# A filter fold in three vector operations for six, and a product unit split by output block, in a gated mix of an FFT convolution and a mixer MLP

## Chip, cores, metric

The kernel runs on one core of a Trainium2 chip. The metric is the device time of one execution in microseconds (us). Five engines work side by side, each through its own list of instructions in order: TensorE (PE in the profile; its weight loads are PEld), VectorE (DVE), ScalarE (ACT), GpSimd (POOL) and SyncE (SP). SP and POOL also issue DMAs; an instruction waits on semaphores for what other engines and DMAs have to finish first.

## What is computed

Two branches over a sequence of S = 2048 rows and D = 640 columns share the input `A_q`, and a gate mixes them. Branch A is a long convolution, branch B a mixer with an MLP. `ssm_k` is a filter of 2048 taps for each of the 640 columns. Cut to what matters:

```python
def A(q, k, v, shift_k, ssm_k, ssm_D):
    k_shift = sum(pad(k, ks-1)[t:t+S] * shift_k[:, ks-1-t] for t in range(ks))   # ks = 4 taps
    kv  = k_shift * v
    y_f = rfft(pad(kv, S)) * rfft(pad(ssm_k, S))      # along the sequence, length 2S
    y   = irfft(y_f)[:S] + kv * ssm_D                 # bf16
    return q * y

def B(x, w1, w2, w3, w4):
    h  = gelu(layernorm(x) @ w1)
    hs = shift_four_column_groups(h, by=(1, -1, 2, -2)) @ w2
    x1 = x + hs
    return x1 + gelu(layernorm(x1) @ w3) @ w4

g   = sigmoid((A_q * gate_w).sum(-1))
out = g * A(A_q, ...) + (1 - g) * B(A_q, ...)
```

## The kernel before

All tensors live in one SBUF arena, so the profile calls nearly every operand `arena`; PSUM is `PSall`. Columns are worked in five chunks of 128 (c = 0 to 4).

Branch A, per chunk. `h_load` brings the filter of 128 columns, `h_fold` adds and subtracts mirrored halves of each block of 512 taps (so that a transform of half the length does), and a DMA transpose turns the result. The skip term `ssm_D` is folded into tap 0 of the filter. `h_even` folds a second time, `h_chunk` multiplies by small DFT matrices on TensorE and ScalarE copies the spectra from PSUM into `HF`. `kv` applies the four taps and the product with v, `kv2` and `x_fwd` do the same transform for the data into `XF`, and `combine` adds neighbouring blocks on VectorE. `x_fwd` has four parts of the spectrum, j = 0 to 3; the operation of `combine` for the lower half reads j = 0 and 1, that for the upper half 2 and 3. `unit(c)` then multiplies the spectra: there are four input blocks and four output blocks, and output block o sums the products over input blocks 0 to o. Complex products are made from three real ones. It works on pairs of output blocks, first (2, 3), then (0, 1): a product of the first filter block, then for each further one a product into `TT` and an addition into `ACC`, and last two operations and one copy of a single row that write the pair back into `XF`. Five of the additions are not VectorE operations but accumulating DMAs issued by POOL, chosen by a table. `final(g, o, q, k)` does the inverse transform on TensorE for a group g of chunks (0 to 2, or 3 and 4) and output block o, mirrors a half by a matmul with a flipped identity, multiplies by q and the gate and stores.

Branch B. `ln1`, `mm1` (w1 and gelu; the four shifted column groups are written into `hT` with their shift, the last 32 columns of each by a small copy), `mm2` (w2; a VectorE operation with PSUM input adds the residual and sums the row, line 980), `ln2`, `mm3` (w3 and gelu), `mm4` (w4, scaled by 1 - g); `base` stores a part of the rows that `mm4` then accumulates into.

What sets the order: the program records all operations with what they read and write, and `schedule` lays them out by `SEQUENCE`, a table of 1171 operation numbers that stands in the program. Each engine executes its operations in that order. `PLACES` gives each PSUM tile its bank. `ON` is a string of choices, one per place where the code calls `turn`: a scaling or a copy of a row on ScalarE or on VectorE, an addition on VectorE or as an accumulating DMA, a copy into `hT` on VectorE or as a DMA. Semaphore waits follow from the recorded dependences alone.

Most VectorE operations are issued by one helper, `tt` (line 660; `ts` is line 665), most ScalarE ones by `act` (670), most matmuls by `mm` (692), nearly all DMAs by line 237. Operations are therefore told apart by their shapes. Those that matter below: the first fold's large operations are 128x1016 (written 128x8x127 in the order), `combine` is 128x1536 (128x3x2x256), `unit` uses 128x2048, 128x1024, 128x3072, 128x1536 and 128x512 operations, `final` 128x256, 128x384, 128x512 and 128x768 ones.

Of the kernel before, what the change touches and what calls it, by code (L numbers as in the profile page):

```python
# [407 lines left out]
def _folded_dft():  # L408
# [22 lines left out]
            np.where(first, np.sin(np.pi * kodd / 2), -np.sin(w * 2 * kodd * p))]  # L431
    alt, one = (-1.) ** p, p == 0
    even[0][:, 0:1], even[1][:, 0:1] = (alt - 1) / 2, 0
    even[2][:, 0:1], even[3][:, 0:1] = one, (alt + 1) / 2
# [12 lines left out]
def bass_gated_mix__ssm_conv_h3__mixer_s_mlp__prompt_kernel(  # L447
# [34 lines left out]
    def ps(n, cls):  # L482
# [3 lines left out]
    SEQUENCE = [1, 4, 5, 6, 26, 7, 3, 45, 24, 8, 0, 49, 50, 51, 55, 48, 68, 9, 10, 11, 12, 13, 14, 15, 16, 69, 17,  # L486
# [682 lines left out]
```

## Time and profile before

| what | value |
|---|---|
| time, median of 3 runs | 221.62 us (221.31 to 222.36) |
| the profiled execution, its own time | 222.27 us |
| its span, first to last instruction | 220.2 us |
| granted TensorE clock, mean | 0.986 |
| VectorE in its first 10 us | 7.53 us busy |
| TensorE in its first 10 us | 6.98 us busy |
| DMA moved | 37.73 MB, mean 171 GB/s |

The profile is of one execution. A row of the groups by form gives line, engine, operation, output and input, shape, count, then busy time and mean duration (ns) of one, then idle time of the engine just before and what ended it. A row of stretches gives start and end, width, and for PE, PEld, DVE, ACT and POOL the busy time and the count, then the granted clock, the DMA share and GB/s. A row in order of time gives start, duration, engine, line and shape; consecutive instructions of one line may be merged into one row. A row of the chain of waits gives start, duration and who held the chain.

### The profile page before, as it was taken

To read this page: it belongs to the slowest core of one execution; us is meant where nothing else is said; L and a number is where in the kernel's file an instruction comes from. 1 tells how busy PE (TensorE), PEld (TensorE's weight loads), DVE (VectorE), ACT (ScalarE), POOL (GpSimd) and SP (SyncE) were. 2 spreads that over 40 slices of the span, in tenths; PEclk is the share of its full clock that TensorE was granted. 3 is DMA by queue.
4 is the path that set the end of the run, shared out by engine and by line. 5 is a ranking of instruction groups with operands and counts; after the bars stand their busy time and mean duration, and the time that the engine had idled before them with its cause. 6 is when DMAs were issued, how large, how long until landed. Compare 5 with 4: busy or idle time off the path is not lost.

```text
span 220.2 us, 3837 instructions
## 1 busy us (share of the span) xinstructions
PE 209.0 (95%) x1401; PEld 125.7 (57%) x1410; DVE 212.1 (96%) x418; ACT 196.5 (89%) x326; POOL 45.7 (21%) x48
## 2 busy tenths in 40 slices
PE   6899999999999999999999999999999999999961
PEld 2598755554664446665446565456665445776730
DVE  5999999999999999999999999999999998999993
ACT  2499999999999999999999999999798978558981
POOL 1331102400010001001380103331101060645440
PEclk9999999999999999999999999999999999999995
DMA  6999998999979995898486893793198299366696
GB/s 170 346 233 214 246 207 231 177 236 193 284 246 204 383 198 95 162 174 185 120 147 110 201 193 43 163 174 71 19 160 182 65 219 246 39 74 71 74 179 119
DMA packets 79440, 37.73 MB, mean 171 GB/s; under 512 B 59001, under 2 KB 76990, under 8 KB 79422
## 3 DMA queue, kind: packets, MB, share of 16 engines
q1 hardware_dynamic: 73920, 31.91, 63.3%
q0 software_dynamic: 5328, 5.51, 18.9%
q8 instruction: 11, 0.18, 0.3%
q10 hardware_dynamic: 174, 0.07, 0.2%
q14 instruction: 7, 0.06, 0.1%
HBM read 14.88 MB, written 5.77 MB: 94 GB/s over the span
## 4 chain that ended last, share of the span: by engine, by line
DVE 57%; PE 28%; DMA 5%; ACT 5%; issue 3%; SPq 0%
DVE arena L660 46%; PE PSall L692 28%; ACT arena L670 5%; DVE arena L665 4%; DMA arena<-arena 3%; DVE arena L861 3%; DVE arena L980 2%; DMA arena<-in_A_q_dram 2%; DVE arena L946 1%; DVE arena L862 0%; DVE arena L866 0%; SPq L237 0%; DVE arena L735 0%; DVE arena L704 0%
## 5 line engine op out<-in xcount | busy, mean ns | idle before, releaser
L692 PE MATMUL PSall<-arena 128*128 128x512 bf16 (+5 forms) x1340 | 201.7, 309 | 3.4 <-ACT arena L670 1.3
L660 DVE TENSOR_TENSOR arena<-arena 128x1024 bf16<-128x1024 bf16 (+14 forms) x270 | 175.1, 712 | 1.7 <-DMA arena<-arena 0.9
L692 PEld LDWEIGHTS PSall<-arena 128*128 128x128 bf16 x1349 | 121.6, 98 | 82.7 <-ACT arena L670 3.3
L670 ACT ACTIVATE arena<-PSall 128x512 bf16<-128x512 f32 (+7 forms) x157 | 94.1, 659 | 9.6 <-PE PSall L750 4.9
L670 ACT ACTIVATE arena<-arena 128x640 bf16<-128x640 bf16 (+5 forms) x107 | 93.5, 904 | 1.9 <-DVE arena L660 1.8
L237 POOL DMA_DIRECT2D out_dram<-arena x24 | 24.1, 1133 | 67.7 <-ACT arena L670 51.7
L869 POOL TENSOR_TENSOR arena<-arena 128x2 f32<-128x2 f32 (+2 forms) x15 | 17.3, 1157 | 58.0 <-DVE arena L866 42.3
L670 ACT ACTIVATE arena<-PSall,arena 128x640 bf16<-128x640 f32 (+2 forms) x32 | 20.5, 652 | 6.8 <-PE PSall L692 6.6
L237 POOL DMA_DIRECT2D arena<-arena x5 | 4.9, 978 | 43.2 <-DVE arena L660 43.2
L980 DVE SCALAR_TENSOR_TENSOR arena<-PSall,arena 128x640 bf16<-128x640 f32 x16 | 12.9, 816 | 0.3
L665 DVE TENSOR_SCALAR arena<-arena 128x640 bf16<-128x640 bf16 (+6 forms) x35 | 11.9, 358 | 0.1
L861 DVE BATCH_NORM_STATS2 arena<-arena 128x6 f32<-128x320 bf16 x20 | 9.0, 484 | 1.3 <-DMA arena<-in_A_q_dram 1.3
L715 PE MATMUL PSall<-arena 128*128 128x512 bf16 x15 | 5.4, 529 | 2.2 <-DVE arena L712 2.2
L670 ACT ACTIVATION_READ_ACCUMULATOR arena<-arena 128x1 f32 x28 | 5.7, 204 | 0.0
L946 DVE TENSOR_SCALAR arena<-arena 32x256 bf16<-32x256 bf16 (+1 forms) x22 | 5.3, 240 | 0.4
L715 PEld LDWEIGHTS PSall<-arena 128*128 128x128 bf16 x15 | 1.8, 128 | 5.0 <-issue 2.5
L922 PE MATMUL PSall<-arena 128*128 128x128 bf16 x40 | 3.4, 220 | 0.9 <-DVE arena L665 0.9
L922 PEld LDWEIGHTS PSall<-arena 128*128 128x128 bf16 x40 | 2.4, 97 | 1.3 <-DVE arena L665 1.3
L866 DVE SCALAR_TENSOR_TENSOR arena<-arena 128x2 f32<-128x2 f32 (+2 forms) x19 | 2.9, 155 | 0.0
L718 ACT ACT_TABLE_LOAD x1 | 1.3, 1283 | 1.3 <-PEq L1154 1.3
L862 DVE BATCH_NORM_AGGREGATE arena<-arena 128x2 f32<-128x12 f32 x10 | 1.7, 192 | 0.0
L980 DVE DVE_READ_ACCUMULATOR arena<-PSall,arena 128x1 f32 x16 | 1.3, 80 | 0.0
(19 smaller groups left out, 2.9 us busy)
## 6 DMA issues: line engine op xcount, KB each, us to landing
arena<-in_A_ssm_k_dram SPq DMA_DIRECT2D x5, 512.0 KB, 5.2
arena<-in_A_q_dram SPq DMA_DIRECT2D x6, 320.0 KB, 5.7
arena<-in_B_w_dram SPq DMA_DIRECT2D x1, 1920.0 KB, 8.4
out_dram<-arena SPq DMA_DIRECT2D x16, 96.0 KB, 3.9
arena<-arena POOLq DMA_DIRECT2D x4, 384.0 KB, 5.0
out_dram<-arena POOLq DMA_DIRECT2D x16, 96.0 KB, 3.6
arena<-in_A_q_dram SPq DMA_DIRECT2D x8, 192.0 KB, 4.1
out_dram<-arena POOLq DMA_DIRECT2D x8, 192.0 KB, 4.0
```

Of the source, the lines that this page charges most:

```text
L237: fn = lambda e: e.dma_start(out, in_, **kw)
L660: P.op(eng, lambda e: e.tensor_tensor(o, real(a), real(b), op), [a, b], [o], dve_ns(o, [a, b], 2) if eng == "dve" else 500)
L665: P.op(eng, lambda e: e.tensor_scalar(o, real(a), s1, s2, op0=op0, **({} if op1 is None else {"op1": op1})), [a] + aps, [o], dve_ns(o, [a] ...
L670: P.op("act", lambda e: e.activation(real(o), real(a), f, bias=bias, scale=scale, **({"accum_out": accum} if accum is not None else {})), ...
L692: fns.append(lambda e, l=l, r=r, i=i: e.matmul(real(o), l, r, start=(i == 0), stop=(i == last)))
L715: P.op("pe", lambda e: e.matmul(real(pw), warm[:, 0:128], warm[:, 128:640], start=True, stop=True), [warm], [pw], 427.0 if i < 14 else 216.0)
L861: P.op("dve", lambda e, o=o, i=i: e.bn_stats(o, i), [i], [o], 400)
L866: P.op("dve", lambda e: e.scalar_tensor_tensor(o, a, x, b, op0=op0, op1=op1), [a, b] + aps, [o], n_of(o) / 0.96 + 65)
L869: P.op("pool", lambda g: g.tensor_tensor(o, a, e, ALU.pow), [a, e], [o], dur)
L922: P.op("pe", [lambda e, c=c, pb=pb, xn=xn: e.transpose(real(pb)[:, 128 * c:128 * (c + 1)], xn[:, 128 * c:128 * (c + 1)], ident) for c in r ...
L946: P.op("dve", lambda e, o=hT[q, 4, c0:c0 + n], i=hx[q, :]: e.tensor_scalar(o, i, 1.0, None, op0=ALU.mult), [hx[q, :]], [hT[q, 4, c0:c0 + n ...
L980: P.op("dve", lambda e: e.scalar_tensor_tensor(x, real(pr), 1.0, x, op0=ALU.mult, op1=ALU.add, accum_out=st[1, 0][:, t:t + 1]), [pr, x], [ ...
```

## The change

`h_fold` had six VectorE operations per chunk: one adds `ssm_D` to tap 0, two each for the sum and the difference (127 columns of eight pieces, and column 128), and one scalar operation that copies column 0 of both halves. Now the sum and the difference take one operation each, over 128 columns of eight pieces, written as one run that starts at element 1; the last column of each piece then falls on column 0 of the next one, and a third operation overwrites those columns and adds `ssm_D`, held in a small tile `skip` with zeros between. The run of the fifth output ends one element beyond the tile, so each chunk's part of the arena is 16 elements longer (`HS`). One column of the difference changes its sign, which two rows of the DFT tables undo. `unit` for the fifth chunk (`LAST`) treats its last pair of output blocks (0, 1) as two single blocks, 1 and then 0. The VectorE copies into `hT` now also name the column beside them as an input. `SEQUENCE` (1163 numbers now), `PLACES` and `ON` are all new.

```diff
+    even[5][0] *= -1
...
+    odd[1][0] *= -1
...
-    SEQUENCE = [1, 4, 5, 6, 26, 7, 3, 45, 24, 8, 0, 49, 50, 51, 55, 48, 68, 9, 10, 11, 12, 13, 14, 15, 16, 69, 17,
...
+    SEQUENCE = [5, 26, 1, 29, 28, 4, 3, 8, 9, 7, 2, 47, 10, 27, 11, 0, 6, 12, 13, 14, 15, 16, 17, 52, 42, 18, 44, 40,
...
-    ON = ("0000000011111111011011111111111100010000010000101111000000000000001000010010000100000100000100000000"
-          "0000000000000000000000000000000")
-
-    HW = S + 4
+    ON = ("0000000011111111111111111111111100010000010000101111000000000000001000010010000100000100000100000000"
+          "00000100000000000000000000000000")
+
+    HW, HS = S + 4, 4096 + 16
...
-    dgT = bfs[:, 32:42]
-    Dcol, gwT = dgT[:, 0:5], dgT[:, 5:10]
+    skip = bfs[:, 0:40].rearrange("p (c e b) -> p c e b", c=5, e=2)
+    gwT = bfs[:, 48:53]
...
+    P.op("dve", lambda e: e.memset(skip, 0.0), [], [skip], 70)
...
-    act(dgT, pr, ACTF.Copy)
+    act(skip[:, :, 1, 0], pr[:, 0:5], ACTF.Copy)
+    act(gwT, pr[:, 5:10], ACTF.Copy)
...
         k, fo = kst[c], kfo[c]
-        tt(k[:, 0, 0:1], k[:, 0, 0:1], Dcol[:, c:c + 1], ALU.add)
         kh = k.rearrange("p b (h i) -> p b h i", h=2)
-        fh = fo.rearrange("p e b (h i) -> p e b h i", h=2)
         for e, op in ((0, ALU.add), (1, ALU.subtract)):
-            tt(fh[:, e, :, :, 1:128], kh[:, :, :, 1:128], kh[:, :, ::-1, 255:128:-1], op)
-            tt(fo[:, e, :, 128], k[:, :, 384], k[:, :, 128], op)
-        ts(fo[:, :, :, 0], kh.rearrange("p b h i -> p h b i")[:, ::-1, :, 0], 1.0, None, ALU.mult)
+            f = fo[:, e, :, 1:129]
+            tt(bass.AP(f.tensor, f.offset, [f.ap[0], [256, 4], [128, 2], [1, 128]]), kh[:, :, :, 1:129], kh[:, :, ::-1, 255:127:-1], op)
+        tt(fo[:, :, :, 0], kh.rearrange("p b h i -> p h b i")[:, ::-1, :, 0], skip[:, c], ALU.add)
...
-                         [hx[q, :]], [hT[q, 4, c0:c0 + n]], n / 3.84 + 65)
+                         [hx[q, :], hT[q, 4, c0 - 1:c0]], [hT[q, 4, c0:c0 + n]], n / 3.84 + 65)
...
-    ADDS = ()
+    ADDS, LAST = (), 4
...
-        for o0 in (2, 0):
-            for a in range(o0 + 2):
+        for o0, o1 in ((2, 4), (0, 2)) if c < LAST else ((2, 4), (1, 2), (0, 1)):
+            for a in range(o1):
                 lo = max(o0, a)
-                n, x0 = o0 + 2 - lo, lo - a
-                acc, tmp = ACC[:, lo - o0:2], TT[:, 0:n]
+                n, x0 = o1 - lo, lo - a
+                acc, tmp = ACC[:, lo - o0:o1 - o0], TT[:, 0:n]
...
-            Y = XF[:, c, o0:o0 + 2]
-            tt(Y[:, :, 0], ACC[:, :, 2], ACC[:, :, 1], ALU.subtract)
-            tt(Y[:, :, 1], ACC[:, :, 2], ACC[:, :, 0], ALU.add)
-            scale(Y[0:1, :, :, 0:128], ACC[0:1, :, 0:2, 0:128], 1.0, True)
+            Y, R = XF[:, c, o0:o1], ACC[:, 0:o1 - o0]
+            tt(Y[:, :, 0], R[:, :, 2], R[:, :, 1], ALU.subtract)
+            tt(Y[:, :, 1], R[:, :, 2], R[:, :, 0], ALU.add)
+            scale(Y[0:1, :, :, 0:128], R[0:1, :, 0:2, 0:128], 1.0, True)
```

Three places of the orders. (All line numbers behind `tt` are higher by one in the changed program.) The first is VectorE at the fold of chunk 0, about 14 us in; BN_STATS and BN_AGGR are the statistics of `ln1`, lines 946 and 947 the copies into `hT`. Before:

```order
L660 TENSOR_TENSOR arena<-arena 128x1
L660 TENSOR_TENSOR arena<-arena 128x4
L946 TENSOR_SCALAR arena<-arena 32x256
L861 BN_STATS arena<-arena 128x6
L665 TENSOR_SCALAR arena<-arena 128x2
L660 TENSOR_TENSOR arena<-arena 128x8x127
L861 BN_STATS arena<-arena 128x6
L660 TENSOR_TENSOR arena<-arena 128x8x127
L665 TENSOR_SCALAR arena<-arena 128x640 x2
L946 TENSOR_SCALAR arena<-arena 32x256
L665 TENSOR_SCALAR arena<-arena 128x8
```

Now:

```order
L862 BN_STATS arena<-arena 128x6 x4
L666 TENSOR_SCALAR arena<-arena 128x640 x2
L947 TENSOR_SCALAR arena<-arena 32x256
L661 TENSOR_TENSOR arena<-arena 128x1024 x2
L863 BN_AGGR arena<-arena 128x2
L661 TENSOR_TENSOR arena<-arena 128x8
```

The fold stands behind four statistics and two normalisations, in one piece, with one operation between its second and third.

The second is VectorE where unit 3 ends and unit 4 begins, about 175 us in. The first row, 128x2x1024, is the product whose sum POOL makes by an accumulating DMA; the last row, 128x2x512, is the first operation that reads that sum. The two 128x3x2x256 are the combines of chunk 4 (before: upper half, then lower; now the same), the 128x384 belong to `final`. Before:

```order
L660 TENSOR_TENSOR arena<-arena 128x2x1024
L660 TENSOR_TENSOR arena<-arena 128x3x2x256
L660 TENSOR_TENSOR arena<-arena 128x384 x2
L660 TENSOR_TENSOR arena<-arena 128x2048
L660 TENSOR_TENSOR arena<-arena 128x3x2x256
L660 TENSOR_TENSOR arena<-arena 128x384
L660 TENSOR_TENSOR arena<-arena 128x4x512
L660 TENSOR_TENSOR arena<-arena 128x384
L660 TENSOR_TENSOR arena<-arena 128x2048
L660 TENSOR_TENSOR arena<-arena 128x2x512
```

Now:

```order
L661 TENSOR_TENSOR arena<-arena 128x2x1024
L661 TENSOR_TENSOR arena<-arena 128x384 x2
L661 TENSOR_TENSOR arena<-arena 128x3x2x256
L661 TENSOR_TENSOR arena<-arena 128x384
L661 TENSOR_TENSOR arena<-arena 128x3x2x256
L661 TENSOR_TENSOR arena<-arena 128x2048
L661 TENSOR_TENSOR arena<-arena 128x384
L661 TENSOR_TENSOR arena<-arena 128x4x512
L661 TENSOR_TENSOR arena<-arena 128x384
L661 TENSOR_TENSOR arena<-arena 128x2048
L661 TENSOR_TENSOR arena<-arena 128x2x512
```

There is one more 128x384 between the product and the reader, and the second combine stands ahead of the 128x2048 that it followed.

The third is ScalarE, in the stretch whose copies the combines of chunk 4 read. The 128x2x4x128 are copies of spectra from PSUM (`h_chunk` and `x_fwd` of chunk 4), the 128x512 the gelus of `mm3`, the 128x384 scalings, the 1x4x128 a row of a unit. Before; the last 128x2x4x128 is the last part of `x_fwd`:

```order
L670 ACTIVATE arena<-PSall 128x2x4x128 x2
L670 ACTIVATE arena<-arena 128x384
L670 ACTIVATE arena<-PSall 128x2x4x128
L670 ACTIVATE arena<-PSall 128x512 x2
L670 ACTIVATE arena<-PSall 128x2x4x128
L670 ACTIVATE arena<-arena 128x384
L670 ACTIVATE arena<-arena 1x4x128
L670 ACTIVATE arena<-PSall 128x2x4x128
```

Now, from the last copy of `h_chunk` to the last of `x_fwd`:

```order
L671 ACTIVATE arena<-PSall 128x2x4x128
L671 ACTIVATE arena<-arena 128x384
L671 ACTIVATE arena<-PSall 128x512 x2
L671 ACTIVATE arena<-PSall 128x2x4x128
L671 ACTIVATE arena<-arena 128x384
L671 ACTIVATE arena<-PSall 128x2x4x128
L671 ACTIVATE arena<-arena 1x4x128
L671 ACTIVATE arena<-PSall 128x512
L671 ACTIVATE arena<-PSall 128x2x4x128
L671 ACTIVATE arena<-PSall 128x512
L671 ACTIVATE arena<-PSall 128x2x4x128
```

The parts of `x_fwd` now stand behind and between four gelus, not two, and on TensorE behind five groups of `mm3` matmuls, not three.

More of the change, by code (lines that the diff above doesn't have):

```diff
@@ L484, in ps @@
         return v if n == 1 else v.rearrange("p (b n) -> p b n", b=2)
-    SEQUENCE = [1, 4, 5, 6, 26, 7, 3, 45, 24, 8, 0, 49, 50, 51, 55, 48, 68, 9, 10, 11, 12, 13, 14, 15, 16, 69, 17,
[59 rows of a table removed]
-    PLACES = [4, 1, 7, 6, 5, 4, 6, 1, 1, 7, 0, 6, 3, 0, 2, 1, 3, 2, 3, 6, 7, 2, 1, 2, 7, 3, 5, 0, 3, 6, 4, 1, 1, 6,
[5 rows of a table removed]
+    SEQUENCE = [5, 26, 1, 29, 28, 4, 3, 8, 9, 7, 2, 47, 10, 27, 11, 0, 6, 12, 13, 14, 15, 16, 17, 52, 42, 18, 44, 40,
[58 rows of a table added]
+    PLACES = [0, 6, 4, 7, 2, 6, 2, 4, 2, 0, 7, 0, 1, 6, 0, 4, 5, 7, 0, 1, 5, 0, 6, 7, 3, 4, 2, 3, 1, 7, 3, 6, 3, 7,
[5 rows of a table added]
                 6, 4]
-    ON = ("0000000011111111011011111111111100010000010000101111000000000000001000010010000100000100000100000000"
-          "0000000000000000000000000000000")
-    HW = S + 4
+    ON = ("0000000011111111111111111111111100010000010000101111000000000000001000010010000100000100000100000000"
+          "00000100000000000000000000000000")
+    HW, HS = S + 4, 4096 + 16
     oXF = alloc(20480)
-    oHF = alloc(20480)
+    oHF = alloc(5 * HS)
     oB = alloc(15360)
@@ L572, in bass_gated_mix__ssm_conv_h3__mixer_s_mlp__prompt_kernel @@
     XF = V(oXF, 20480).rearrange("p (c b r n) -> p c b r n", c=5, b=4, r=2)
-    HF = V(oHF, 20480).rearrange("p (c b r n) -> p c b r n", c=5, b=4, r=2)
+    HF = [V(oHF + HS * c, 4096).rearrange("p (b r n) -> p b r n", b=4, r=2) for c in range(5)]
     hT = V(oHT, DC * HW).rearrange("p (c s) -> p c s", c=DC)
@@ L598, in bass_gated_mix__ssm_conv_h3__mixer_s_mlp__prompt_kernel @@
     four = lambda o: V(o, 2048).rearrange("p (e b k c) -> p e b k c", e=2, b=4, k=2)
-    kst = [V(oHF + 4096 * c, 2048).rearrange("p (b n) -> p b n", b=4) for c in range(5)]
-    kfo = [V(oHF + 4096 * c + 2048, 2048).rearrange("p (e b n) -> p e b n", e=2, b=4) for c in range(5)]
+    kst = [V(oHF + HS * c, 2048).rearrange("p (b n) -> p b n", b=4) for c in range(5)]
+    kfo = [V(oHF + HS * c + 2048, 2048).rearrange("p (e b n) -> p e b n", e=2, b=4) for c in range(5)]
     KT = [V(oXF + 4096 * c, 2048) for c in range(5)]
     VT = [V(oXF + 4096 * c + 2048, 2048) for c in range(5)]
-    TD = [V(oHF + 4096 * c + 2048, 2048) for c in range(5)]
-    TA, TB = V(oB + 8192, 2048), [V(oHF + 4096 * c, 2048) for c in range(5)]
+    TD = [V(oHF + HS * c + 2048, 2048) for c in range(5)]
+    TA, TB = V(oB + 8192, 2048), [V(oHF + HS * c, 2048) for c in range(5)]
     sdT = [four(oXF + 16384 if c < 4 else oHF) for c in range(5)]
     het = [four(oXF + 18432 if c < 4 else oHF + 2048) for c in range(5)]
-    evn = [V(oHF + 16384 if c < 4 else oHF + 4096, 2048).rearrange("p (o e b c) -> p o e b c", o=2, e=2, b=4) for c in range(5)]
-    eft = [V(oHF + 18432 if c < 4 else oHF + 6144, 2048).rearrange("p (m e b c) -> p m e b c", m=2, e=2, b=4) for c in range(5)]
+    evn = [V(oHF + 4 * HS if c < 4 else oHF + HS, 2048).rearrange("p (o e b c) -> p o e b c", o=2, e=2, b=4) for c in range(5)]
+    eft = [V(oHF + 4 * HS + 2048 if c < 4 else oHF + HS + 2048, 2048).rearrange("p (m e b c) -> p m e b c", m=2, e=2, b=4) for c in range(5)]
     ACC, TT = [V(oB + 3072 * i, 3072).rearrange("p (o m n) -> p o m n", o=2, m=3) for i in range(2)]
@@ L613, in bass_gated_mix__ssm_conv_h3__mixer_s_mlp__prompt_kernel @@
     pair = lambda o, n: V(o, 2 * n).rearrange("p (t d) -> p t d", t=2)
-    qA = [pair(oHF + 8192 + 768 * k if k < 5 else oHF + 4096 + 768 * (k - 5), 384) for k in range(8)]
-    qB = [pair(oHF + 12288 + 512 * k, 256) for k in range(8)]
+    qA = [pair(oHF + 2 * HS + 768 * k if k < 5 else oHF + HS + 768 * (k - 5), 384) for k in range(8)]
+    qB = [pair(oHF + 3 * HS + 512 * k, 256) for k in range(8)]
     abA = [pair(oW2 + 768 * i, 384) for i in range(4)]
@@ L618, in bass_gated_mix__ssm_conv_h3__mixer_s_mlp__prompt_kernel @@
     abB = [pair(oB + 8192 + 512 * i, 256) for i in range(8)]
-    gyB = [pair(oHF + 16384 + 512 * i, 256) for i in range(8)]
+    gyB = [pair(oHF + 4 * HS + 512 * i, 256) for i in range(8)]
     sm = V32(oSm, 388)
@@ L796, in h_chunk @@
                 mm(pr[:, r, :], pairs)
-            act(HF[:, c, :, :, 128 * j:128 * (j + 1)].rearrange("p b r d -> p r b d"), pr.rearrange("p r (b c) -> p r b c", b=4), ACTF.Copy)
+            act(HF[c][:, :, :, 128 * j:128 * (j + 1)].rearrange("p b r d -> p r b d"), pr.rearrange("p r (b c) -> p r b c", b=4), ACTF.Copy)
     def k_load(c):
@@ L1013, in mm4 @@
         P.dma("pool", out[0, 128 * t:128 * (t + 1), 0:NA], X[:, t, 0:NA], accum=True)
-    ADDS = ()
+    ADDS, LAST = (), 4
     def unit(c):
-        X4, H4 = XF[:, c], HF[:, c]
+        X4, H4 = XF[:, c], HF[c]
         tt(SX, X4[:, :, 0], X4[:, :, 1], ALU.add)
```

127 rows, old and new, of tables (PLACES, SEQUENCE) are left out of this document.

## The prediction

> **What bounds the kernel now.** I read the busy table of the page first, then busy time by stretches, then the groups by form, then the chain of waits and the time order at the places that the change touches.
>
> ```profile
> span 220.2 us, 3837 instructions
> PE 209.0 (95%) x1401; PEld 125.7 (57%) x1410; DVE 212.1 (96%) x418; ACT 196.5 (89%) x326; POOL 45.7 (21%) x48
> 20.00:60.00 40.00, 39.64 (x293) 24.08 (x296) 39.53 (x97) 39.62 (x73) 5.84 (x5) 1.00 1.03 221
> 60.00:100.00 40.00, 39.84 (x237) 23.24 (x239) 39.59 (x63) 39.95 (x57) 2.08 (x2) 1.00 0.95 210
> 100.00:140.00 40.00, 39.89 (x222) 21.71 (x223) 39.75 (x57) 39.76 (x60) 9.94 (x8) 1.00 0.73 141
> 140.00:180.00 40.00, 39.89 (x231) 22.66 (x232) 39.97 (x59) 36.73 (x50) 9.56 (x11) 1.00 0.65 131
> 180.00:212.00 32.00, 31.57 (x225) 21.52 (x223) 31.00 (x63) 25.00 (x48) 12.59 (x12) 1.00 0.74 109
> 212.00:217.00 5.00, 1.33 (x5) 0.32 (x4) 4.84 (x18) 2.86 (x6) 1.19 (x1) 0.72 0.90 170
> L692 PE MATMUL PSall<-arena 128*128 128x512 bf16 x48 | 10.5, 379 | 0.0
> ```
>
> From 20 to 212 us TensorE (first pair behind the width of a stretch) is idle 192 - 190.83 = 1.2 us and VectorE (third pair) 192 - 189.84 = 2.2 us. The last row is TensorE from 100 to 110 us, 48 matmuls of 128x512 without idle time at the granted clock of 1.00: 0.22 us each, so this busy time is streaming, not waiting. Both engines are full, and neither has two microseconds to give. The rest of the span is the start, and the tail, where from 212 us VectorE alone is full (4.84 of 5.00) and TensorE waits for it. An edit that shortens VectorE's work alone is stopped by TensorE wherever the two hand over, and what it shortens in the tail comes out whole.
>
> **The change part by part.** First the price of one VectorE instruction, in the forms that come and go.
>
> ```profile
> L660 DVE TENSOR_TENSOR arena<-arena 128x1024 bf16<-128x1024 bf16 x80 | 52.0, 682 | 1.0 <-DMA arena<-arena 0.9
> L660 DVE TENSOR_TENSOR arena<-arena 128x2048 bf16<-128x2048 bf16 x40 | 48.1, 1214 | 0.1
> L660 DVE TENSOR_TENSOR arena<-arena 128x1536 bf16<-128x1536 bf16 x16 | 15.1, 947 | 0.2 <-ACT arena L670 0.2
> L660 DVE TENSOR_TENSOR arena<-arena 128x512 bf16<-128x512 bf16 x22 | 9.0, 417 | 0.1
> L660 DVE TENSOR_TENSOR arena<-arena 128x384 bf16<-128x384 bf16 x16 | 5.4, 348 | 0.0
> L660 DVE TENSOR_TENSOR arena<-arena 128x1016 bf16<-128x1016 bf16 x10 | 6.7, 680 | 0.0
> L660 DVE TENSOR_TENSOR arena<-arena 128x4 bf16<-128x4 bf16 x10 | 1.6, 166 | 0.0
> L660 DVE TENSOR_TENSOR arena<-arena 128x1 bf16<-128x1 bf16 x5 | 0.8, 150 | 0.0
> L665 DVE TENSOR_SCALAR arena<-arena 128x8 bf16<-128x8 bf16 x5 | 0.9, 181 | 0.0
> L665 DVE TENSOR_SCALAR arena<-arena 128x640 bf16<-128x640 bf16 x16 | 6.6, 430 | 0.0
> L946 DVE TENSOR_SCALAR arena<-arena 32x256 bf16<-32x256 bf16 x15 | 3.3, 219 | 0.2
> L946 DVE TENSOR_SCALAR arena<-arena 32x512 bf16<-32x512 bf16 x7 | 2.0, 287 | 0.1
> 14.67 0.69 DVE L660 TENSOR_TENSOR arena<-arena 128x1016 bf16<-128x1016 bf16 x1
> 15.28 0.48 DVE L861 BATCH_NORM_STATS2 arena<-arena 128x6 f32<-128x320 bf16 x1
> 17.34 0.19 DVE L665 TENSOR_SCALAR arena<-arena 128x8 bf16<-128x8 bf16 x1
> 17.42 0.21 DVE L946 TENSOR_SCALAR arena<-arena 32x256 bf16<-32x256 bf16 x1
> 18.01 0.18 DVE L660 TENSOR_TENSOR arena<-arena 128x4 bf16<-128x4 bf16 x1
> 18.09 0.49 DVE L861 BATCH_NORM_STATS2 arena<-arena 128x6 f32<-128x320 bf16 x1
> ```
>
> The last six rows show that an instruction's duration is not its price: the one of 128x1016 takes 0.69 us and the next starts after 0.61, those of 128x8 and 128x4 take 0.19 and 0.18 and the next starts after 0.08. Some 0.08 us of each lies under its successor, so I price a form at its mean less 0.08.
>
> *The fold.* Per chunk go two operations of 128x1016, two of 128x4, one of 128x1 and the scalar one of 128x8; two of 128x1024 and one of 128x8 come. A large one costs 0.60 either way (680 and 682 ns). So three small ones fewer per chunk, 15 in all, at 0.08: -1.2 us. With their whole durations (10 x 0.166 + 5 x 0.150 + 5 x 0.181, less five at about 0.17) it would be -2.5, the lower bound; -0.9 is the upper, if the new third operation, which must wait for the two before it, hides nothing behind them. I take -1.2.
>
> *The split of unit 4.* One 128x2048 and three 128x1024 go, two 128x1024 and six 128x512 come: 2 x 0.60 + 6 x 0.34 - 1.13 - 3 x 0.60 = +0.3 us on VectorE (+0.6 by whole durations).
>
> *Moved onto VectorE by the new table of choices.* One scaling of 128x384, between the 0.22 of 32x256 and the 0.43 of 128x640, taken at 0.27; one copy of 32x256 and one of 32x512 into hT, at their 0.22 and 0.29, because their neighbours wait for them: +0.8 us, between +0.6 and +0.95. What leaves is a ScalarE scaling and two issues on SyncE's queue. ScalarE also gets one more copy of a few elements and one more short row scaling, some 0.2 to 0.8 us; it is idle 220.2 - 196.5 = 23.7 us, 7 of them from 180 to 212 us, so I count nothing. One small memset is +0.1.
>
> VectorE's work is thus -1.2 + 0.3 + 0.8 + 0.1 = 0.0 us, between -1.6 and +0.9. TensorE's list of matmuls is the same. So the order alone decides, by the waits that it removes and adds. Four places count.
>
> *The accumulating DMA of unit 3.*
>
> ```profile
> 176.97 6.79 DMA arena<-arena
> ...
> 183.78 1.83 DVE L660 TENSOR_TENSOR arena<-arena 128x1024 bf16<-128x1024 bf16 x2 [0.89 <-DMA arena<-arena]
> arena<-arena POOLq DMA_DIRECT2D x4, 384.0 KB, 5.0
> ```
>
> Here is VectorE's only long wait of the middle, 0.89 us. The first row is a piece of the chain: the DMA is issued at 176.97 and has landed 6.79 us later. The product that feeds it has left VectorE at 176.60 (next fence), so the way through the DMA took 7.2 us. Between that product and the operation that reads the sum VectorE has rows for 2 x 0.87 + 4 x 0.27 + 3 x 1.13 = 6.2 us. The new order puts one more 128x384 there, 6.5 us, and it puts both combines of chunk 4 there (before, too). If the transfer takes its 6.8 again, 0.6 to 0.7 of the wait stays; at the median of 5.0 (last row) nothing stays. The gain is 0.2 to 0.9.
>
> *The combine of chunk 4.* It needs the copies of the last forward matmuls.
>
> ```profile
> 174.73 1.00 ACT L670 ACTIVATE arena<-PSall 128x1024 bf16<-128x1024 f32 x1
> 176.60 0.95 DVE L660 TENSOR_TENSOR arena<-arena 128x1536 bf16<-128x1536 bf16 x1
> 179.14 0.94 DVE L660 TENSOR_TENSOR arena<-arena 128x1536 bf16<-128x1536 bf16 x1
> ```
>
> The last copy ends at 175.73, and the combine that reads it starts at 179.14: 3.4 us to spare. Now five groups of mm3, not three, stand ahead of that copy and less of mm4; summing the order's matmuls ahead of it (0.22 us for 512 columns, in proportion for the rest) puts it 2.2 us later, and summing VectorE's rows puts its reader 2.1 us earlier. The spare time is gone: a wait of up to 3.4 - 4.3 = 0.9 us, and 0.2 more at the first combine. Queued behind it on VectorE is unit 4, and behind that the tail. But the same wait is cover for the DMA above, so it costs only what exceeds the 0.6 left there: 0 to +0.5. Together with the DMA the place is worth -0.9 to +0.5, and I take -0.2.
>
> *The last sums of mm2.*
>
> ```profile
> 66.66 0.59 PE L692 MATMUL PSall<-arena 128*128 128x512 bf16 x2
> 66.91 1.22 DVE L660 TENSOR_TENSOR arena<-arena 128x2048 bf16<-128x2048 bf16 x1
> 68.12 0.82 DVE L980 SCALAR_TENSOR_TENSOR arena<-PSall,arena 128x640 bf16<-128x640 f32 x1
> ```
>
> TensorE has passed the last mm2 matmul at 66.66, and its reader starts at 68.12, 1.2 us behind what it needs. In the new orders that matmul stands at the same sum of work, and its reader 1.4 us earlier on VectorE: a wait of 0 to 0.3, I take 0.1. VectorE's saving up to here is thus mostly stopped by TensorE, as the two full rows above let expect.
>
> *The tail.* The outputs of o = 1 no longer wait for those of o = 0. VectorE's rows behind the last product are 10.1 us, not 12.5. That could remove the little waiting in the tail (VectorE's 0.16 of 5.00 in the last row of stretches and part of 32 - 31.0 - 0.89), 0.2 us, and the shorter drain; against it the order ends with one flip matmul whose result VectorE awaits with 0.8 us of rows to cover some 1.2, +0.4. I take -0.1, between -0.5 and +0.4.
>
> The sum: 0.0 - 0.2 + 0.1 - 0.1 = -0.2 us. The profiled execution took 222.27 us (its span of 220.2 and 2.1 around it), so it becomes 222.1. The median of the runs is 221.62; I put the same -0.2 on it, **221.4 us**.
>
> A rule of the Trainium skill speaks against the fold (VectorE: DVE Perf Modes, section on the walkthrough of the 8-slice pipeline): two elements per cycle ask for step 1 or -1 and 4-byte alignment, and the new operations write from an odd element on. The row of 128x1016 has the same odd first elements and takes 680 ns, no more than the 682 of the aligned form, so the trace disagrees; by the rule the ten operations would lose the rate that they have.
>
> **The rivals.** (1) *The waits go and no new one comes*: the transfer takes its median, the second combine finds its copy ready because TensorE runs earlier than its place says, the small operations' durations count in part (-1.6), and the tail gains: -0.7 (work) - 0.7 - 0.4 = -1.8, 219.8 us. For it: ScalarE and TensorE need to be only 1 us earlier at chunk 4, and the start, where TensorE idles 0.86 us for VectorE ahead of one transpose, may improve. Against it: from 20 to 212 us TensorE has 1.2 us of idle time to give.
>
> ```profile
> 8.56 0.45 PE L922 MATMUL PSall<-arena 128*128 128x128 bf16 x5 [0.86 <-DVE arena L665]
> ```
>
> (2) *Slower: the combine of chunk 4 waits for the forward transform.* From the point where TensorE or the copies run more than 1 us later there than now, the wait exceeds what the DMA hides; at 2 us late it is 0.9 + 0.2 + 1.0 - 0.6 = +1.5, all of VectorE's remaining 33 us moves with it, and +0.2 comes from the flip: 223.3 us. For it: the margin of 3.4 us vanishes by the orders alone. Against it: the orders show no other place that makes TensorE later. (3) *The fold falls to one element per cycle*, the rule above as a mechanism: between 128x512 and 128x1024 a form costs (682 - 417)/512 = 0.52 ns per element, so half the rate adds 0.53 us to each of ten operations, +5.3 us, 226.9. The 680 ns speak against it.
>
> **How the numbers follow.** Forecast 0.45, rival 1 0.30, rival 2 0.20, rival 3 0.02, the rest either way. Faster or slower by over 0.5% means over 1.1 us, about what a measurement of this kernel can tell from no change. Rival 1 is faster; rivals 2 and 3 slower; of the forecast, whose own range by the bounds is 220.3 to 222.7, 0.03 is faster and 0.02 slower: 0.33, 0.43, 0.24. The range must reach both rivals' figures: 219.5 to 223.4.
>
> **What would show it.** VectorE's busy time within 1 us of 212.1; ten operations of 128x1024 at 680 ns in place of the 128x1016; no wait of 0.9 us for the DMA of unit 3, but VectorE waiting for ScalarE at a combine near 177 us; TensorE's busy time unchanged. The forecast is wrong if TensorE's idle time between 20 and 212 us grows by more than 1 us, or if VectorE's last operation leaves 217 us by more than 1 us.

## The result, and the profile after

The changed kernel takes 220.11 us (median of 5 runs, 219.82 to 220.21) against 221.62 us before: ratio 0.992, 95% interval 0.9902 to 0.9939. It is faster by 1.5 us by the medians, 1.8 us by the ratio. The forecast was 221.4, no change; what came is next to the first rival, 219.8.

The page of the changed kernel, and its busy time by the stretches that the prediction used (start and end, width, then PE, PEld, VectorE, ScalarE and POOL):

```profile
span 218.0 us, 3825 instructions
PE 208.8 (96%) x1400; PEld 126.2 (58%) x1410; DVE 211.7 (97%) x411; ACT 196.9 (90%) x328; POOL 46.5 (21%) x48
20.00:60.00 40.00, 39.51 (x295) 23.99 (x296) 39.49 (x93) 39.28 (x72) 5.45 (x5) 1.00 1.06 227
60.00:100.00 40.00, 39.90 (x237) 23.07 (x237) 39.71 (x62) 39.94 (x57) 3.00 (x2) 1.00 0.95 206
100.00:140.00 40.00, 39.84 (x221) 21.83 (x223) 39.90 (x57) 39.25 (x59) 8.69 (x7) 1.00 0.59 123
140.00:180.00 40.00, 39.90 (x230) 22.50 (x231) 39.93 (x55) 36.63 (x50) 11.10 (x13) 1.00 0.84 151
180.00:212.00 32.00, 30.70 (x224) 21.52 (x221) 31.92 (x72) 26.27 (x52) 12.46 (x12) 1.00 0.74 113
212.00:217.00 5.00, 1.07 (x3) 0.31 (x3) 3.29 (x13) 1.42 (x3) 0.75 (x1) 0.58 0.84 173
```

From 20 to 212 us VectorE now idles 192 - 190.95 = 1.05 us (2.2 before), TensorE 192 - 189.85 = 2.15 us (1.2 before). VectorE has become the fuller of the two, but only behind 180 us, where TensorE idles 1.30 of 32 us. From 60 to 180 us both are full: VectorE idles 0.46 us and TensorE 0.36 us. The chain that ended last, as the page gives it by engine, before and after, does not single out VectorE either:

```profile
DVE 57%; PE 28%; DMA 5%; ACT 5%; issue 3%; SPq 0%
```

```profile
PE 72%; DVE 17%; ACT 5%; DMA 3%; issue 2%
```

VectorE's longest wait behind 20 us is this, at a sum of mm2, and the places that the prediction spoke of look like this (rows in order of time, cut out one by one: the copy that the second combine of chunk 4 reads, that combine, the first reader of unit 3's accumulated sum, VectorE's last operation, the last store):

```profile
64.86 0.82 DVE L981 SCALAR_TENSOR_TENSOR arena<-PSall,arena 128x640 bf16<-128x640 f32 x1 [0.29 <-PE PSall L693]
...
175.58 1.02 ACT L671 ACTIVATE arena<-PSall 128x1024 bf16<-128x1024 f32 x1
176.69 0.95 DVE L661 TENSOR_TENSOR arena<-arena 128x1536 bf16<-128x1536 bf16 x1
181.50 0.68 DVE L661 TENSOR_TENSOR arena<-arena 128x1024 bf16<-128x1024 bf16 x1
215.19 0.29 DVE L661 TENSOR_TENSOR arena<-arena 128x256 bf16<-128x256 bf16 x1
215.51 0.34 SPq L237 DMA_DIRECT2D out_dram<-arena  x1
```

(A wait in brackets is shown from 0.15 us on.) The 0.89 us for unit 3's DMA are gone: the reader has no wait in brackets. The copy for the combine ends at 176.60 and the combine starts at 176.69: no time to spare, as predicted, but no wait either. The last two rows answer to these of before:

```profile
216.45 0.87 SPq L237 DMA_DIRECT2D out_dram<-arena  x2
216.66 0.29 DVE L660 TENSOR_TENSOR arena<-arena 128x256 bf16<-128x256 bf16 x1
```

VectorE ends at 215.48 instead of 216.95, 1.47 us earlier, and from there to the end of the span it is 218.0 - 215.48 = 2.5 us instead of 220.2 - 216.95 = 3.2. That makes the 2.2 us between the two spans. VectorE's 1.47 are its busy time, 212.1 to 211.7 = -0.4, and its idle time, which is 216.95 - 212.1 = 4.9 before and 215.48 - 211.7 = 3.8 after, -1.1, of which the DMA wait is 0.9. The profiled execution of before (222.27 us) was 0.65 us slower than its median, that of the change (219.82) 0.29 us faster, so 2.2 us overstate what the medians show.

The new order covers unit 3's DMA a little better, but the transfer itself was also shorter. From its issue to its landing, before and after:

```profile
arena<-arena POOLq DMA_DIRECT2D x1, 384.0 KB, 6.8
```

```profile
arena<-arena POOLq DMA_DIRECT2D x1, 384.0 KB, 5.8
```

From the issue (175.38) to the reader (181.50) it is 6.1 us, 0.2 more than the 5.9 that VectorE had without its wait before, so at 6.8 us a wait of 0.7 would have stayed. In the profiles of all runs below the same transfer takes 5.5 to 5.8 us in the new order and 5.9 to 6.8 in the old one; why is open.

### The profile page after: what moved, and what is told of

Same layout as the page of the kernel before. It is cut to its first block, busy times and chain, and to the rows that moved or that the text cites. A ratio compares the mean times of both kernels' runs of the same rounds, so it can differ in the third digit from the quotient of the medians.

```text
span 218.0 us, 3825 instructions
## 1 busy us (share of the span) xinstructions
PE 208.8 (96%) x1400; PEld 126.2 (58%) x1410; DVE 211.7 (97%) x411; ACT 196.9 (90%) x328; POOL 46.5 (21%) x48
## 4 chain that ended last, share of the span: by engine, by line
PE 72%; DVE 17%; ACT 5%; DMA 3%; issue 2%
PE PSall L693 72%; DVE arena L661 8%; ACT arena L671 5%; DVE arena L862 4%; DVE arena L666 3%; DMA arena<-arena 2%; DVE arena L947 1%; DMA arena<-in_A_q_dram 1%; DVE arena L863 0%; DVE arena L737 0%; DVE arena L981 0%; DVE arena L867 0%
## 5 line engine op out<-in xcount | busy, mean ns | idle before, releaser
L693 PE MATMUL PSall<-arena 128*128 128x256 bf16 (+5 forms) x1339 | 201.1, 309 | 3.5 <-DVE arena L661 2.4
L661 DVE TENSOR_TENSOR arena<-arena 128x1024 bf16<-128x1024 bf16 (+11 forms) x264 | 174.3, 725 | 0.6
L671 ACT ACTIVATE arena<-arena 128x640 bf16<-128x640 bf16 (+6 forms) x107 | 94.1, 910 | 1.0 <-DMA arena<-arena 0.5
L237 POOL DMA_DIRECT2D out_dram<-arena x24 | 24.7, 1235 | 37.6 <-ACT arena L671 19.8
L717 PE MATMUL PSall<-arena 128*128 128x512 bf16 x15 | 6.7, 584 | 2.0 <-DVE arena L714 2.0
L947 DVE TENSOR_SCALAR arena<-arena 32x256 bf16<-32x256 bf16 (+1 forms) x24 | 5.8, 242 | 0.5
L671 ACT ACTIVATION_READ_ACCUMULATOR arena<-arena 128x1 f32 x28 | 6.2, 221 | 0.0
```

Source lines behind the costliest of these rows:

```text
L237: fn = lambda e: e.dma_start(out, in_, **kw)
L661: P.op(eng, lambda e: e.tensor_tensor(o, real(a), real(b), op), [a, b], [o], dve_ns(o, [a, b], 2) if eng == "dve" else 500)
L671: P.op("act", lambda e: e.activation(real(o), real(a), f, bias=bias, scale=scale, **({"accum_out": accum} if accum is not None else {})), ...
L693: fns.append(lambda e, l=l, r=r, i=i: e.matmul(real(o), l, r, start=(i == 0), stop=(i == last)))
L717: P.op("pe", lambda e: e.matmul(real(pw), warm[:, 0:128], warm[:, 128:640], start=True, stop=True), [warm], [pw], 427.0 if i < 14 else 216.0)
L947: P.op("dve", lambda e, o=hT[q, 4, c0:c0 + n], i=hx[q, :]: e.tensor_scalar(o, i, 1.0, None, op0=ALU.mult), [hx[q, :], hT[q, 4, c0 - 1:c0]] ...
```

## The experiments

Theory A: VectorE sets the end, so the change gains what VectorE's work and waits lose. Against it stand, in the expectations: B, TensorE's start decides; C, the gain is the fold's; D, what VectorE saves is stopped at hand-overs to TensorE; and for single parts E to H. Every run was timed beside the kernel before on the same chip; ratios are to that kernel, with 95% intervals. Orders are changed by giving every operation of the one program its place in the other's `SEQUENCE`, with that program's `PLACES`.

**1. The new order with the old operations.**

```diff
-    ADDS, LAST = (), 4
+    ADDS, LAST = (), 5
...
-            tt(bass.AP(f.tensor, f.offset, [f.ap[0], [256, 4], [128, 2], [1, 128]]), kh[:, :, :, 1:129], kh[:, :, ::-1, 255:127:-1], op)
+            tt(fh[:, e, :, :, 1:128], kh[:, :, :, 1:128], kh[:, :, ::-1, 255:128:-1], op)
+            tt(fo[:, e, :, 128], k[:, :, 384], k[:, :, 128], op)
```

> The changed kernel's order and banks with the operations of before: six operations per fold, unit 4 unsplit, the three choices (two hT copies, one 128x384 scaling) off VectorE. Theory A (the end is VectorE's work plus its waits; the new order takes the 0.9 us wait for unit 3's DMA away and adds none): the operations weigh -1.2 + 0.3 + 0.8 + 0.1 = 0.0 against each other, so this runs like the changed kernel, 220.1 us (219.7 to 220.7), no VectorE wait over 0.3 us between 170 and 185 us. Theory C (the gain is the fold's three operations fewer): it loses the gain and stands near before, 221.3 to 221.8 us.

223.65 us, ratio 1.0093 (1.0079 to 1.0107): slower than before, against both theories. VectorE's waits in its trace:

```profile
46.17 0.82 DVE L982 SCALAR_TENSOR_TENSOR arena<-PSall,arena 128x640 bf16<-128x640 f32 x1 [1.54 <-PE PSall L692]
...
206.59 2.03 DVE L660 TENSOR_TENSOR arena<-arena 128x384 bf16<-128x384 bf16 x7 [0.66 <-ACT arena L670]
208.91 10.17 DVE L660 TENSOR_TENSOR arena<-arena 128x768 bf16<-128x768 bf16 x35 [0.29 <-ACT arena L670]
```

2.5 us of waits that neither kernel has. The order without its operations is worse than the old order.

**2. The old order with the new operations.**

```diff
-    SEQUENCE = [5, 26, 1, 29, 28, 4, 3, 8, 9, 7, 2, 47, 10, 27, 11, 0, 6, 12, 13, 14, 15, 16, 17, 52, 42, 18, 44, 40,
+    SEQUENCE = [1, 2, 5, 6, 7, 27, 8, 4, 47, 25, 9, 0, 51, 52, 53, 57, 50, 70, 10, 11, 12, 13, 14, 15, 16, 17, 71,
```

> The order and banks of before with all the new operations (three per fold, unit 4 split with its second part behind its first, the three choices on VectorE). Theory A: VectorE's work is about the same and the wait for unit 3's DMA stays, 221.2 to 221.8 us, the wait 0.5 to 1.5 us. Theory C: the gain is here, 219.9 to 220.5 us.

223.27 us, ratio 1.0076 (1.0062 to 1.0089). Its order of the split half is mine (block 0 directly behind block 1), and VectorE waits in the tail:

```profile
200.63 5.57 DVE L662 TENSOR_TENSOR arena<-arena 128x768 bf16<-128x768 bf16 x14 [0.36 <-ACT arena L672]
206.90 11.39 DVE L662 TENSOR_TENSOR arena<-arena 128x384 bf16<-128x384 bf16 x40 [0.70 <-ACT arena L672]
```

So neither set helps alone in this form, and the parts are tested below each inside one order.

**3. The reader of unit 3's sum later, in before.**

```diff
-                ..., 784, 926, 945, 1156, 1093, 1094, 1036, 791, ...
+                ..., 926, 945, 1156, 1093, 1094, 1036, 791, 784, ...
```

> Before, with one thing moved: VectorE's first reader of unit 3's accumulated sum stands behind the next product (128x2048, 1.13 us) and not ahead of it. Theory A: the wait of 0.9 us goes and the time with it, 220.5 to 221.0 us. Theory B (TensorE paces, and a wait that leaves this place comes back at the next hand-over; the gain of the change is TensorE's earlier start): no change, 221.3 to 221.9 us, with VectorE waiting 0.5 us or more for TensorE or ScalarE behind 185 us.

222.35 us, ratio 1.0035 (1.0022 to 1.0048). The wait did not go, it moved to the product that I had put ahead:

```profile
184.09 1.23 DVE L660 TENSOR_TENSOR arena<-arena 128x2048 bf16<-128x2048 bf16 x1 [0.69 <-DMA arena<-arena]
```

That product writes `TT`, the buffer that the DMA still reads. What counts as cover is the work ahead of the first operation that needs either the sum or the buffer. The run tells nothing of A or B. Nor is its slower time shown to come from the move. A sum of mm2 at 60 us, before and in this run:

```profile
60.13 0.82 DVE L980 SCALAR_TENSOR_TENSOR arena<-PSall,arena 128x640 bf16<-128x640 f32 x1
```

```profile
60.63 0.82 DVE L980 SCALAR_TENSOR_TENSOR arena<-PSall,arena 128x640 bf16<-128x640 f32 x1 [0.30 <-PE PSall L692]
```

In the profile VectorE is 0.5 us late there already, over 100 us ahead of what was moved. Why is open.

**4 and 12. TensorE late, in the changed kernel.** Four more matmuls of 128x512 ahead of the first product of mm1 (0.9 us), or ten (2.2 us), into a bank that nothing reads.

```diff
-        P.op("pe", lambda e: e.matmul(real(pw), warm[:, 0:128], warm[:, 128:640], start=True, stop=True),
+        P.op("pe", [lambda e: e.matmul(real(pw), warm[:, 0:128], warm[:, 128:640], start=True, stop=True)] * (5 if i == 14 else 1),
```

> The changed kernel with four more warm-up matmuls of 128x512 just ahead of the first mm1 product, so that TensorE does 0.9 us more before the same work. Theory A: VectorE hides it but for the start, 220.1 to 220.4 us, no new wait at the combine of chunk 4. Theory B: TensorE's 1.0 us lead is what kept the combine of chunk 4 from waiting, so VectorE waits 0.5 to 0.9 us for ScalarE's copy near 176 us and the time rises to 220.6 to 221.0 us.

> The changed kernel with ten more warm-up matmuls of 128x512 (2.2 us of TensorE) ahead of the first mm1 product. Theory A: TensorE makes most of it good in idle time before and behind, 220.2 to 220.8 us. Theory B (what the prediction feared: the combine of chunk 4 has no time to spare, so TensorE's delay beyond the 0.9 us of the smaller run comes out there and at the other hand-overs): 221.1 to 222.0 us, with VectorE waits of over 0.5 us for TensorE or ScalarE.

220.18 us (ratio 0.9933, 0.9921 to 0.9945) and 221.36 us (0.9972, 0.996 to 0.9985): the first 0.9 us cost nothing that can be told, ten matmuls cost 1.2. But B's place is wrong. Rows of the run with ten:

```profile
66.61 0.82 DVE L981 SCALAR_TENSOR_TENSOR arena<-PSall,arena 128x640 bf16<-128x640 f32 x1 [0.29 <-PE PSall L693]
...
177.33 1.02 ACT L671 ACTIVATE arena<-PSall 128x1024 bf16<-128x1024 f32 x1
178.45 0.95 DVE L661 TENSOR_TENSOR arena<-arena 128x1536 bf16<-128x1536 bf16 x1
216.94 0.29 DVE L661 TENSOR_TENSOR arena<-arena 128x256 bf16<-128x256 bf16 x1
```

The wait at the mm2 sum is 0.29 us in both kernels, only 1.75 us later (66.61 against 64.86), the combine finds its copy ready again, and VectorE ends 1.75 us later (217.23 against 215.48). From that sum to VectorE's end it is 150.62 us in both. In the profile with four matmuls that sum stands at 65.42 and VectorE ends at 215.93, so there too the delay is only in part made good. So up to 65 us TensorE sets the pace; what delays TensorE early holds VectorE back too, and the two reach the combine in step. From there VectorE runs its own length, but TensorE is as full up to 180 us, and these runs do not tell which of the two decides between 65 and 180 us.

**5. The old fold in the changed kernel.**

```diff
-            tt(bass.AP(f.tensor, f.offset, [f.ap[0], [256, 4], [128, 2], [1, 128]]), kh[:, :, :, 1:129], kh[:, :, ::-1, 255:127:-1], op)
-        tt(fo[:, :, :, 0], kh.rearrange("p b h i -> p h b i")[:, ::-1, :, 0], skip[:, c], ALU.add)
+            tt(fh[:, e, :, :, 1:128], kh[:, :, :, 1:128], kh[:, :, ::-1, 255:128:-1], op)
+            tt(fo[:, e, :, 128], k[:, :, 384], k[:, :, 128], op)
+        ts(fo[:, :, :, 0], kh.rearrange("p b h i -> p h b i")[:, ::-1, :, 0], 1.0, None, ALU.mult)
```

> The changed kernel with the six-operation fold of before; nothing else differs (the three more operations per chunk stand directly at the new ones' places). Theory A: VectorE is the engine that sets the end, so its work counts in full: 15 small operations at 0.08 us, +1.2 us, 221.1 to 221.6 us. Theory D (TensorE paces the middle; VectorE's small savings vanish at the hand-overs): at most +0.4, 219.9 to 220.5 us.

220.64 us, ratio 0.9935 (0.9919 to 0.9952), 0.5 us above the changed kernel by the medians, with intervals that overlap. Page, the sum of mm2 that waited 0.29 us in the changed kernel with the row ahead of it, and VectorE's last operation:

```profile
PE 208.3 (95%) x1400; PEld 125.8 (58%) x1410; DVE 212.3 (97%) x426; ACT 197.0 (90%) x328; POOL 46.2 (21%) x48
...
64.83 0.08 DVE L982 DVE_READ_ACCUMULATOR arena<-PSall,arena 128x1 f32 x1
65.06 0.82 DVE L982 SCALAR_TENSOR_TENSOR arena<-PSall,arena 128x640 bf16<-128x640 f32 x1
215.49 0.29 DVE L660 TENSOR_TENSOR arena<-arena 128x256 bf16<-128x256 bf16 x1
```

VectorE's busy time is 212.3 - 211.7 = 0.6 us more, and its end comes 0.3 us later (215.78). The wait at that sum is halved: the row ahead ends at 64.91, so 0.15 us of it are left. Up to the sum, with three of the five folds, VectorE is 0.2 us later (65.06 against 64.86), and behind it, with the other two, 0.1 us more. So about half of what the old fold adds fills idle time, of which 0.14 us is the wait for TensorE: neither A nor D alone. The page's chain has VectorE at 77% here and TensorE at 72% in the changed kernel, with 0.4 us between the spans: the two are too close for the chain to name one.

**6. Without the split.** The changed kernel with `LAST = 5`.

```diff
-    ADDS, LAST = (), 4
+    ADDS, LAST = (), 5
```

> The changed kernel with unit 4's last half in one piece again (both output blocks' products, sums and outputs together); order, fold and choices as changed. VectorE's work falls by 0.3 us. Theory A with the tail of the order-only run (there VectorE waited 0.7 and 0.3 us for ScalarE behind 206 us): the two waits appear here too and the time is +0.4 to +1.2, 220.5 to 221.3 us. Theory E (the split is only a cost, the waits of the order-only run came from its other parts): 219.6 to 220.0 us.

221.2 us, ratio 0.997 (0.9957 to 0.9982), disjoint from the changed kernel's. The two waits of the first run are here:

```profile
204.15 2.03 DVE L661 TENSOR_TENSOR arena<-arena 128x384 bf16<-128x384 bf16 x7 [0.66 <-ACT arena L671]
206.47 10.17 DVE L661 TENSOR_TENSOR arena<-arena 128x768 bf16<-128x768 bf16 x35 [0.29 <-ACT arena L671]
```

E falls. VectorE's busy time is 211.8 us without the split and 211.7 with it: the split costs nothing, and in the new order it removes 0.95 us of waiting for ScalarE in the tail.

**7. The fold alone, in before.** As in 5, the other way round, in the order of before.

> Before's order, banks, choices and unsplit unit 4, with the three-operation fold alone. Theory A: 15 small operations fewer on VectorE, -1.2 us, 220.3 to 220.7 us (before ran at 221.65 on this chip). Theory D: the saved time is stopped at hand-overs to TensorE, 221.2 to 221.8 us.

221.39 us, ratio 0.9978 (0.9964 to 0.9993): 0.5 us, between the two. Page and the group of the fold:

```profile
PE 208.8 (95%) x1401; PEld 126.0 (57%) x1410; DVE 211.3 (96%) x404; ACT 196.2 (89%) x327; POOL 45.6 (21%) x48
...
L661 DVE TENSOR_TENSOR arena<-arena 128x1024 bf16<-128x1024 bf16 x90 | 58.8, 683 | 0.4 <-DMA arena<-arena 0.3
```

The ten new operations do not raise the mean (683 ns, 682 before). VectorE's busy time is 0.8 us under the 212.1 of before.

**8. Two sums behind unit 3's last product, in before.**

```diff
-                ..., 774, 937, 957, 986, 722, 723, 1008, 775, ..., 778, 782, 935, 936, 735, 1021, 987, ...
+                ..., 774, 937, 957, 722, 723, 775, ..., 778, 782, 935, 936, 735, 986, 1008, 1021, 987, ...
```

> Before, with two operations of 128x384 (sums of the last stage, 0.27 us each) moved from ahead of unit 3's last product to behind the first combine of chunk 4: the accumulating DMA starts 0.54 us earlier and has 0.54 us more VectorE work over it, ahead of the first operation that needs its sum or its buffer. Theory A: the wait of 0.9 us falls to 0.3 to 0.5 and the time by 0.5, 220.9 to 221.4 us. Theory D: the wait falls and the time stays, 221.5 to 221.9 us.

221.47 us, ratio 0.9978 (0.9966 to 0.9991). One row of VectorE, seventeen operations without a wait over the place of the old one:

```profile
175.00 11.51 DVE L660 TENSOR_TENSOR arena<-arena 128x2048 bf16<-128x2048 bf16 x17
```

The wait is gone altogether, not only by 0.54, and the time falls by 0.5 us by the ratio (0.33 by the medians). A holds here: this waiting of VectorE comes out as time. The times show less of it than the 0.89 us in the profile of before, which was of an execution 0.65 us above the median; in run 7's profile, with the same order, the wait is 0.34 us.

**9 and 10. The choices, in the changed kernel.** The 128x384 scaling back on ScalarE; or the two copies into `hT` back to DMAs.

```diff
-          "00000100000000000000000000000000")
+          "00000000000000000000000000000000")
...
-    ON = ("0000000011111111111111111111111100010000010000101111000000000000001000010010000100000100000100000000"
+    ON = ("0000000011111111011011111111111100010000010000101111000000000000001000010010000100000100000100000000"
```

> The changed kernel with the one 128x384 scaling (near 110 us) back on ScalarE. Theory A (VectorE's work counts): -0.25 us, 219.7 to 220.0 us. Theory F (ScalarE, which has under 0.1 us of idle time between 66 and 100 us and 0.7 between 100 and 140, is as full there and passes its longer work on): 220.2 to 220.6 us.

> The changed kernel with the two copies into hT (32x256 near 28 to 33 us, 32x512 near 40 us) as DMAs on SyncE's queue again, as before the change; the order of the rest is the changed one. VectorE's work falls by 0.5 us. Theory G (in the new order these DMAs land too late; they are what made the order-only run wait 1.5 us for TensorE at 46 us): VectorE idles 1.5 to 2.5 us between 20 and 60 us and the time is 221.3 to 222.6 us. Theory A without such a wait: 219.6 to 219.9 us.

The scaling: 220.66 us, ratio 0.9939 (0.9917 to 0.9962), which overlaps the changed kernel's; no gain. The trace shows where the saving went, as F says. VectorE near 130 us, in the changed kernel and in this run:

```profile
126.91 6.51 DVE L661 TENSOR_TENSOR arena<-arena 128x2048 bf16<-128x2048 bf16 x8
```

```profile
132.00 1.23 DVE L662 TENSOR_TENSOR arena<-arena 128x2048 bf16<-128x2048 bf16 x1 [0.22 <-ACT arena L672]
```

VectorE does one operation less at 110 us (0.27 us as the prediction prices it) and waits 0.22 us for ScalarE at 132 us, where the changed kernel runs through. The copies: 222.33 us, ratio 1.0025 (1.0003 to 1.0046), and G is right: TensorE waits for a DMA, then VectorE for TensorE:

```profile
44.31 2.95 PE L694 MATMUL PSall<-arena 128*128 128x320 bf16 x17 [0.98 <-DMA arena<-arena]
...
45.86 0.82 DVE L982 SCALAR_TENSOR_TENSOR arena<-PSall,arena 128x640 bf16<-128x640 f32 x1 [1.31 <-PE PSall L694]
```

**11. Fold and sums, in before.** The edits of 7 and 8 in one kernel.

> Before's order with the three-operation fold and with the two 128x384 sums behind unit 3's last product: the fold-alone run and the sums-behind run in one. Theory A (both act on VectorE, and add up): -0.4 and -0.35 by the two medians, 220.8 to 221.2 us, no wait for unit 3's DMA over 0.2 us. Theory H (both take the same waiting time, so the second brings nothing): 221.3 to 221.6 us. In both cases 0.7 us or more stays to the changed kernel, which would be the end behind VectorE's last operation (3.1 to 3.4 us in the profiles with before's order, 2.5 to 2.8 with the new one).

220.99 us, ratio 0.9959 (0.9943 to 0.9975; one of its twelve executions took 1246.79 us and does not move the median): the median lies where A has it and not H, so the two add up, though the three ratios' intervals overlap. Its end, behind the last operation of VectorE, is that of before's order, 219.3 - 216.08 = 3.2 us:

```profile
span 219.3 us, 3832 instructions
215.79 0.29 DVE L661 TENSOR_TENSOR arena<-arena 128x256 bf16<-128x256 bf16 x1
```

No version beat the changed kernel.

## Why the prediction was wrong in its forecast and right in its range

The gain of 1.5 us by the medians (1.8 by the ratio) is made of three parts. The fold gives 0.4 to 0.5 (run 7), the DMA wait 0.3 to 0.5 (run 8), 0.9 to 1.0 together (run 11). The rest, 0.5 by the medians and 0.9 by the ratios, fits the shorter end behind VectorE's last operation: 2.5 to 2.8 us in the eight profiles with the new order, 3.1 to 3.4 in the six with the old one. That last part is read from profiles only; nothing was run that changes it alone. Of its 0.6 us, 0.35 is a pause of POOL after the last store has landed, between its last two semaphore instructions (first and last start, before and after):

```profile
L1139 POOLq EVENT_SEMAPHORE  x2: 17/17/17, 219.6 to 220.1; - x2
```

```profile
L1140 POOLq EVENT_SEMAPHORE  x2: 17/17/17, 217.8 to 217.9; - x2
```

It is 0.4 us in all six profiles with the old order and 0.1 in all eight with the new one; its cause is open. The split and the copies gain nothing against before: they remove waits that the new order would have.

The range held by its width. The forecast's own bounds, 220.3 to 222.7, miss 220.11, which lies in the range (219.5 to 223.4) only because that reaches past rival 1.

*What bounds the kernel.* Right: up to the mm2 sums TensorE (runs 4 and 12), and from there both are full. "What it shortens in the tail comes out whole" was not tested in the tail itself. Ahead of it a saving on VectorE comes out here and not there: the wait at 183 us did (run 8), the scaling at 110 us did not (run 9).

*The fold, -1.2.* The mechanism was right, the size not. VectorE's busy time falls by 0.8 us (run 7), 0.05 us for each of the 15 small operations and not 0.08, a little beyond the upper bound of -0.9; of that 0.5 reaches the time. The prediction said itself that savings up to the mm2 sums are mostly stopped by TensorE, and counted the fold's first three chunks in full all the same.

*The split, +0.3.* 0.0 on VectorE, and its use, 1.1 us in this order, was not seen: the tail's waits were looked for in the old order alone, where there are none.

*The choices, +0.8.* For the two copies the wrong question was asked. Not what they cost VectorE, but what their DMAs would cost in the new order: 2.2 us.

*VectorE's work in sum, 0.0.* -0.4, inside the bounds. Added up from the parts, these are -1.5 and +0.75, not -1.6 and +0.9.

*Unit 3's DMA and the combine of chunk 4, together -0.2.* This is the step that failed. The gain of the wait was in its bounds (0.89 in the profile, 0.3 to 0.5 in time), helped by a transfer of 5.8 us and not 6.8. The cost beside it, a wait of up to 0.9 us at the combine, did not come: the copy ended 0.9 us later than before (176.60 against 175.73), not "2.2 us later", while its reader came 2.45 us earlier (176.69 against 179.14), not 2.1. The sum over the order's matmuls left out what TensorE waits at the start. Its busy time in that stretch, before and after:

```profile
7.00:20.00 13.00, 11.97 (x184) 10.42 (x182) 12.86 (x49) 11.10 (x36) 3.06 (x5) 1.00 1.05 266
```

```profile
7.00:20.00 13.00, 12.91 (x180) 11.17 (x179) 12.76 (x45) 12.36 (x37) 3.74 (x5) 1.00 0.96 270
```

1.0 us of idle time became 0.1, so TensorE came to the forward transform 0.9 us ahead of what its place says; that accounts for 0.9 of the 1.3 us by which the sum was off, and the other 0.4 stay with the sum itself. But a better start is not why the combine did not wait. In run 12 TensorE is late again, and the combine still starts 0.1 us behind its copy (178.45 against 177.33 + 1.02): VectorE is held at the mm2 sum and shifts too. The prediction summed each engine's work for itself and left this hand-over out. So a late start of TensorE does not make rival 2's wait.

Rival 1 named both conditions (TensorE 1 us earlier, the start improves). That its 219.8 lies so near is in part luck: its work of -0.7 does not follow from its own terms, -1.6 + 0.3 + 0.8 + 0.1 = -0.4, with which it comes to 220.1.

*The last sums of mm2, +0.1.* A wait of 0.29 us came, at the top of the 0 to 0.3.

*The tail, -0.1.* VectorE runs through it without a wait over 0.15 us and the end behind it is 0.6 shorter; "the shorter drain" was named and not sized, and the bound of -0.5 was too narrow. The split is not what shortens the end: it is 2.7 us without the split (run 6) and 3.1 with the split in the old order (run 2).

*Rival 3, the rate of the fold.* It did not happen. The rule in the Trainium skill (VectorE: DVE Perf Modes, the walkthrough of the 8-slice pipeline) asks for 4-byte alignment for two elements per cycle. The trace of run 7 disagrees: ten operations from an odd element at half the rate (0.53 us more each, as the prediction has it) would lift the mean of the 90 to 741 ns, and it is 683.

*What was to show it.* VectorE's busy time within 1 us, the fold at 680 ns and TensorE's busy time came as said; VectorE's wait at a combine near 177 us did not come. By its own test the forecast is wrong: VectorE's last operation was to stay within 1 us of 217 and ends at 215.48.

## What to carry to other kernels

A sum of work ahead of an instruction gives its time only with the idle time of that engine counted too. To tell whether one engine will wait for another, sum both from the last place where one was held by the other. Where an order was made together with its operations, price an operation by the wait that comes without it in that order; either half alone can be slower, as in runs 1 and 2. A buffer that a DMA still reads holds back its next writer as much as the sum holds back its reader.

## What had not been expected of the hardware

Taking 15 operations of 0.15 to 0.18 us away freed 0.8 us, 0.05 us each, though each seemed to take 0.08 from one start to the next. The time from VectorE's last operation to the end of the span depends on the order, by 0.6 us, with the same last store, and more than half of that is POOL's pause after all work is done. Moving one reader behind a product (run 3) made the kernel 0.35% slower (0.22 to 0.48), with 0.5 us lost ahead of the place that was changed. The accumulating DMA of unit 3, 384 KB each time, took 5.5 to 5.8 us in one order and 5.9 to 6.8 in the other. The cause of all three is open.
